# Hashed attention with a convolved feed-forward layer: reciprocals spread by two transposes, and queries and keys loaded head by head

## The chip, the cores and the metric

The kernel runs on one core of a Trainium2 chip. A core has a matmul engine (PE, with its weight loads shown apart as PEld), a vector engine (DVE), a scalar engine (ACT), a general engine (POOL) and a queue for transfers (SP). Each works through its own instructions in order, and semaphores tie them together. The metric is the device time of one execution in microseconds (us); lower is better.

## The reference

Four batches of eight heads, 768 positions, head size 64. Queries and keys are hashed to six sign bits; a query attends only to keys of its own bucket. The attention's output, the heads side by side, goes through a feed-forward layer with a convolution over three positions that gates the hidden values.

```python
q_bits = (np.einsum('bhsd,dk->bhsk', q, proj) > 0).astype(np.int64)
...
mask = q_bucket[:, :, :, None] == k_bucket[:, :, None, :]
scores = scale * np.matmul(q, k.transpose(0, 1, 3, 2))
scores = np.where(mask, scores, -1000000000.0)
scores = scores - np.max(scores, axis=-1, keepdims=True)
attn = np.exp(scores)
attn = attn / (np.sum(attn, axis=-1, keepdims=True) + 1e-09)
return np.matmul(attn, v).astype(np.float32)
...
h = np.maximum(x @ w_in, 0.0)
...
    conv_out += conv_w[k][None, None, :] * hp[:, k:k + S, :]
gate = 1.0 / (1.0 + np.exp(-conv_out))
return (h * gate @ w_out).astype(np.float32)
```

## The kernel before

Heads are worked on in pairs: sixteen pairs (`Pair`), four per batch. A pair has twelve units (`Unit`), each 128 queries of one head against all 768 keys. After the last pair of a batch, three pairs delayed (`DEFER`), comes that batch's feed-forward stage (`ffn`).

A unit goes through four steps. `products` (L257): the scores, in four matmuls into a PSUM tile `s`; the values are split into a high and a low part, and the hash bits ride along as additional rows, so that a wrong bucket gives a large negative score. `maximum` (L270): DVE copies the scores to `e` and takes their maximum. `exponential` (L277): ACT. `transposes` (L297), three units later (`LAG`): PE turns `e`, six blocks of 128 x 128, into a PSUM tile `t`, and ACT copies it to `at` (L304). The tiles `s` and `t` (and that of the hash) are taken in turn from three PSUM buffers, the ring `S`.

Four units make a block of 256 queries for both heads. Its product with the values, `values`, is done in one go behind the last unit of the following block: `spread`, then six chunks for each head (L325). The first seven pairs divide by the sum of the exponentials only there: `reciprocals` (L291, L292) makes four reciprocals per partition on DVE, two units ahead of the burst, and `spread` (L319) turns them into rows, by matmuls with `ident` in which each reciprocal is read 64 times; ACT copies the result to `rs`, and DVE multiplies (L333). The later pairs (`late`) divide each unit's `e` on POOL and have no `spread`.

While a pair runs, the next is prepared. `load` brings R, queries and keys of both heads (L158), with one buffer. `hash` (L186) computes the bits on PE and DVE (L189); `split` makes the high part `hi` on POOL (L171), the low part in place of R (L176), and SP copies both to the tiles that the products read (L174, L178; the target that the profile names `k<-R` is K2). In the main loop, with `k` the unit within the pair, `split` does its four steps at k = 1, 3, 5 and 7, the hash is at k = 3, and at k = 7 SP gets `load_v` for the next pair and then `load` for the one after it. A load of R waits until all readers of the buffer are done, the copies included.

In the background of the first pairs, DVE, ACT and POOL decode the weights of the feed-forward stage, which arrive as 64-bit numbers (L91 to L112), some five steps in each burst.

All the order is written out by hand: each engine has its instructions in the order of the main loop.

Of the kernel before, what the change touches and what calls it, by code (L numbers as in the profile page):

```python
# [17 lines left out]
P = 128  # L18
# [14 lines left out]
LATE = NP + DEFER  # L33
AVS = (1 + NCK, 0, 0, 0)
PREP = 1
PREP_N = 6
W0 = 7
RATE = 5.2
WC = 512
# [3 lines left out]
def lsh_attention_conv_ffn(ctx, tc, qk, v, hw, w_in, conv_w, w_out, consts, ident_in, out):  # L43
# [100 lines left out]
    class Pair:  # L144
        def __init__(self, b, p):
            self.b, self.p, self.nm = b, p, f"{b}_{p}"
            self.late = b * NP + p >= LATE
            self.inv = None

        def load(self):  # L150
            nm = self.nm
            self.R = ring(wp, 1, [P, 2, S], F32R, "R", f"R{nm}")
            src = qk[self.b, 2 * self.p:2 * self.p + 2].rearrange("h p s -> p h s")
            if self.b == self.p == 0:
                for h in range(2):
                    nc.sync.dma_start(self.R[:, h].bitcast(F32), src[:, h])
            else:
                nc.sync.dma_start(self.R.bitcast(F32), src)  # L158
            self.Q1 = ring(wp, 2, [P, 2, S], F32R, "Q1", f"Q1{nm}")
            self.K1 = ring(wp, 2, [P, 2, S], F32R, "K1", f"K1{nm}")  # L160
            self.Q2, self.K2 = Q2s[self.p % 2], K2s[self.p % 2]
# [4 lines left out]

        def split(self, h):

            lo, R = self.R[:, h], self.R[:, h].bitcast(F32)
            hi = ring(wp, 1, [P, S], F32R, "hi", f"hi{self.nm}_{h}")  # L170
            nc.gpsimd.tensor_scalar(hi, R, 1.0, 0.0, ALU.mult, ALU.add)  # L171
            for dst, src in ((self.Q1[:64, h], hi[:64]), (self.Q2[:64, h], hi[:64]),
                             (self.K1[:64, h], hi[64:]), (self.K1[64:, h], hi[64:])):
                nc.sync.dma_start(dst.bitcast(F32), src.bitcast(F32))  # L174
            yield
            nc.gpsimd.tensor_tensor(lo, R, hi.bitcast(F32), ALU.subtract)  # L176
            for dst, src in ((self.Q1[64:, h], lo[:64]), (self.K2[:64, h], lo[64:])):
                nc.sync.dma_start(dst.bitcast(F32), src.bitcast(F32))  # L178

        def hash(self):  # L180
            hp = ring(ps, 3, [P, 2, 512], F32, "S", f"hash{self.nm}")
            R = self.R.bitcast(F32)
            for h in range(2):
                for half in range(2):
                    g = 32 * (2 * h + half)
                    nc.tensor.matmul(hp[g:g + 32, 0, :HS], hw_sb[:, :32], R[:, h, half * HS:(half + 1) * HS],  # L186
                                     start=True, stop=True, tile_position=(0, g))
# [22 lines left out]
        def prepare_now(self):  # L210

            nm = self.nm
            hps = []
            for h in range(2):
                hps.append(ring(ps, 2, [P, 512], F32, "M", f"hash{nm}_{h}")[:, :HS])
                for g in range(4):
                    c, half = 32 * (1 + g // 2), g % 2
                    nc.tensor.matmul(hps[h][32 * g:32 * g + 32], hw_sb[:, c:c + 32],
                                     self.R[:, h, half * HS:(half + 1) * HS].bitcast(F32),
                                     start=True, stop=True, tile_position=(0, 32 * g))  # L220
            for h in range(2):
                R = self.R[:, h].bitcast(F32)
                Q1, Q2, K1, K2 = (t[:, h] for t in (self.Q1, self.Q2, self.K1, self.K2))
                nc.gpsimd.tensor_scalar(K1[64:], R[64:], 1.0, 0.0, ALU.mult, ALU.add)
                nc.scalar.copy(K1[:64], R[64:])
                nc.vector.tensor_copy(Q1[:64], R[:64])
                nc.scalar.copy(Q2[:64], R[:64])
                nc.vector.tensor_tensor(Q1[64:], R[:64], Q1[:64].bitcast(F32), ALU.subtract)
                if h == 1:
                    yield  # L230
                bits = ring(wp, 4, [P, WC], I32, "w", f"bits{nm}_{h}").bitcast(F32)[:, :HS]
                nc.vector.tensor_scalar(bits, hps[h], 0.0, cst[:, 2:3], ALU.is_gt, ALU.subtract)
                nc.vector.tensor_tensor(K2[:64], R[64:], K1[64:].bitcast(F32), ALU.subtract)
                for g, dst in enumerate((K2, K2, Q2, Q2)):
                    p, dst = slice(32 * g, 32 * g + 32), dst[64:96, g % 2 * HS:(g % 2 + 1) * HS]
                    if g % 2 == 0:
                        nc.scalar.activation(dst, bits[p], AF.Copy, scale=cst[p, 3:4])  # L237
                    else:
                        nc.gpsimd.tensor_scalar(dst, bits[p], cst[p, 3:4], 0.0, ALU.mult, ALU.add)
            yield  # L240
            nc.vector.tensor_copy(K2s[1][64:96], zero[64:96])
            nc.vector.tensor_copy(Q2s[1][64:96], zero[64:96])


    class Unit:
# [41 lines left out]
        def reciprocals(self):  # L287

            pr = self.pair
            pr.inv = ring(wp, 2, [P, 2 * QB // P], F32, "inv", f"inv{self.nm}")  # L290
            nc.vector.tensor_reduce(pr.inv, self.sums, mybir.AxisListType.X, ALU.add)  # L291
            nc.vector.reciprocal(pr.inv, pr.inv)  # L292

        def transposes(self):
            self.tp = ring(ps, 3, [P, 2, 512], F32, "S", f"t{self.nm}")
# [11 lines left out]
    def values(pr, qb, ats, inv):  # L307
# [7 lines left out]
        def spread():  # L315

            for t in range(QB // P):
                for h in range(2):
                    nc.tensor.matmul(av[h * D:(h + 1) * D, QB + t * P:QB + (t + 1) * P],  # L319
                                     inv[:, 2 * t + h:2 * t + h + 1].to_broadcast([P, D]), ident,  # L320
                                     start=True, stop=True, tile_position=(0, h * D))

        def chunk(c):
            for h in range(2):
# [87 lines left out]
    def ffn(b, xs, fill, last):  # L412
# [4 lines left out]
        for i in range(len(todo) + FLAG):  # L417
# [17 lines left out]
            if i < len(todo):  # L435
# [3 lines left out]
    pairs = [Pair(b, p) for b in range(B) for p in range(NP)]  # L439
    units = [Unit(pr, t, h) for pr in pairs for qb in range(S // QB) for h in range(2)  # L440
             for t in range(qb * QB // P, (qb + 1) * QB // P)]
    pairs[0].load()
    nc.sync.dma_start(ident, ident_in)
    pairs[0].load_v()
    cwr = cp.tile([P, 2 * NFC * 3], I32, name="cwr")
    nc.sync.dma_start(cwr, conv_w)
    first = pairs[0].prepare_now()
    next(first)
    pairs[1].load()
    av, outs, lows, early = [], [], [], None  # L450
    n = len(units)
    ffn_after = {min((b + 1) * NP - 1 + DEFER, B * NP - 1): b for b in range(B)}
    for i in range(n + LAG):
# [53 lines left out]
        for last in parts:  # L507
            last()
        prepare(1)
        if u and k == PREP + PREP_N and pi + 1 < len(pairs):  # L510
            pairs[pi + 1].load_v()
            if pi + 2 < len(pairs):
                pairs[pi + 2].load()
        if i == 3:
            taps.append(decode_taps(cwr))
        for g in taps:
# [64 lines left out]
```

## Time and profile before

| | us |
|---|---|
| median of 3 runs | 740.17 |
| lowest, highest | 739.85, 744.33 |
| profiled execution, whole | 739.48 |
| its span, first to last instruction | 737.5 |

A row of the profile names the line of the code, the engine, the operation, the tile written and those read, and the number of instructions; behind a bar stand the busy time in us, the mean of one in ns, and the idle time of the engine just before, with what ended it. PE's ends are modelled, since matmuls overlap: for them the distance from start to start counts.

| stage, us from the start | what runs |
|---|---|
| 0 to 28 | first pair, loads, start of the decoding |
| 28 to 224 | pairs that use `spread`; decoding of the weights |
| 224 to 290 | feed-forward stage of the first batch |
| 290 to 396 | pairs that divide on POOL |
| 396 to 737.5 | the same by turns: feed-forward, pairs, feed-forward, pairs, feed-forward |

### The profile page before, as it was taken

What the parts mean: (1) busy time and instruction counts of PE and PEld (TensorE: products, weight loads), DVE (VectorE), ACT (ScalarE), POOL (GpSimd) and SP (SyncE); (2) the same over time, 40 slices, a digit from 0 to 9 for tenths busy, and PEclk for the clock granted to TensorE, in tenths of its full rate; (3) what the DMA queues carried; (4) which work ended last, traced back from release to release, by engine and by line L of the source; (5) the groups of instructions that cost most, each with busy time, mean ns of one, the idle gap of its engine ahead of it and who ended that gap; (6) DMA issues with size and microseconds to landing.
All of it is one profiled execution on the core that took longest, in us unless ns stands there. A gap on an engine that the chain in (4) does not pass through costs nothing.

```text
span 737.5 us, 13543 instructions
## 1 busy us (share of the span) xinstructions
PE 710.9 (96%) x4720; PEld 589.0 (80%) x4720; DVE 487.3 (66%) x1211; ACT 498.5 (68%) x937; POOL 331.9 (45%) x334
## 2 busy tenths in 40 slices
PE   6998999899899999999999999999999999999997
PEld 3787777678778988777877998778778899878996
DVE  7977878788775755666665666466666566555663
ACT  5788578678684554877877554778778655585554
POOL 4265456357463522475673532355755232241321
PEclk9999999999999999999999999999999999999999
DMA  4867666663552310237545130324463001100011
GB/s 143 222 187 202 165 186 166 165 166 89 147 146 52 86 44 36 72 77 189 139 105 149 34 94 3 108 60 113 117 180 95 1 0 44 44 1 1 0 44 43
DMA packets 30355, 72.17 MB, mean 98 GB/s; under 512 B 5936, under 2 KB 7504, under 8 KB 30288
## 3 DMA queue, kind: packets, MB, share of 16 engines
q1 hardware_dynamic: 27696, 62.88, 32.0%
q10 hardware_dynamic: 2592, 8.44, 3.3%
q8 instruction: 37, 0.61, 0.3%
q14 instruction: 30, 0.25, 0.1%
HBM read 27.40 MB, written 6.29 MB: 46 GB/s over the span
## 4 chain that ended last, share of the span: by engine, by line
PE 69%; DMA 11%; POOL 7%; issue 5%; DVE 4%; SPq 3%; ACT 1%; POOLq 0%; DVEq 0%; ACTq 0%
PE h L368 19%; PE o L398 18%; PE v L325 11%; PE s L257 10%; PE t L297 9%; DMA R<-in_qk 6%; DMA k<-R 4%; POOL R L176 2%; SPq L174 2%; DVE e L270 1%; DMA K<-hi 1%; PE hash L186 1%; POOL hi L171 1%; ACT e L277 1%; SPq L178 1%
## 5 line engine op out<-in xcount | busy, mean ns | idle before, releaser
L270 DVE TENSOR_SCALAR_CACHE_REDUCE e<-s 128x768 f32<-128x768 f32 x192 | 183.2, 954 | 81.2 <-PE s L257 70.6
L277 ACT ACTIVATE e<-e,st 128x768 f32<-128x768 f32 x192 | 181.3, 944 | 10.3 <-DVE st L284 5.0
L304 ACT COPY at<-t 128x768 f32<-128x768 f32 x192 | 152.3, 794 | 47.0 <-PE t L297 47.0
L297 PE MATMUL t<-ident,e 128*128 128x128 f32 x1152 | 160.0, 275 | 3.6 <-POOL e L285 1.5
L377 DVE SCALAR_TENSOR_TENSOR ht<-ht,cw 128x384 f32<-128x384 f32 (+1 forms) x128 | 114.7, 896 | 71.2 <-ACT ht L375 69.0
L387 POOL TENSOR_TENSOR g<-ht,g 128x384 fp32r<-128x384 f32 x64 | 71.5, 1117 | 179.5 <-ACT g L386 141.8
L297 PEld LDWEIGHTS t<-ident,e 128*128 128x128 f32 x1152 | 130.6, 141 | 22.3 <-POOL e L285 7.4
L285 POOL TENSOR_SCALAR e<-e,st 128x768 f32<-128x768 f32 x108 | 98.3, 911 | 103.1 <-DVE st L284 51.4
L398 PE MATMUL o<-wo,g 128*128 128x512 f32 x576 | 142.4, 394 | 0.0
L368 PE MATMUL h<-xh,wi 128*128 128x386 f32 x512 | 141.9, 340 | 0.0
L325 PE MATMUL v<-at,v 128*64 128x256 f32 x1152 | 135.6, 385 | 0.0
L398 PEld LDWEIGHTS o<-wo,g 128*128 128x128 f32 x576 | 107.4, 188 | 20.3
L257 PE MATMUL s<-K,Q 128*128 128x384 f32 x384 | 116.7, 385 | 1.9 <-ACT e L277 1.0
L325 PEld LDWEIGHTS v<-at,v 128*64 128x64 f32 x1152 | 81.2, 138 | 42.4 <-issue 8.6
L257 PE MATMUL s<-k,q 96*128 96x384 f32 x384 | 100.2, 342 | 2.1 <-ACT q L237 1.9
L368 PEld LDWEIGHTS h<-xh,wi 128*128 128x128 f32 x512 | 94.1, 188 | 4.8 <-issue 1.8
L380 ACT ACTIVATE ht<-ht 128x384 f32<-128x384 f32 x64 | 33.6, 526 | 91.4 <-DVE ht L377 91.4
L368 PE MATMUL h<-xl,wi 128*128 128x386 f32 x256 | 86.7, 339 | 0.0
L257 PEld LDWEIGHTS s<-K,Q 128*128 128x128 f32 x384 | 59.0, 192 | 23.2 <-issue 16.6
L257 PEld LDWEIGHTS s<-k,q 96*128 96x128 f32 x384 | 70.7, 191 | 3.5 <-ACT q L237 3.0
L381 DVE TENSOR_TENSOR ht<-ht 128x384 f32<-128x384 f32 x64 | 40.2, 629 | 33.4 <-ACT ht L380 33.4
L176 POOL TENSOR_TENSOR R<-R,hi 128x768 fp32r<-128x768 f32 x30 | 56.6, 1886 | 0.2
(75 smaller groups left out, 586.0 us busy)
## 6 DMA issues: line engine op xcount, KB each, us to landing
R<-in_qk SPq DMA_DIRECT2D x15, 768.0 KB
K<-hi SPq DMA_DIRECT2D x60, 192.0 KB
v<-in_v SPq DMA_DIRECT2D x16, 384.0 KB
out<-osb SPq DMA_DIRECT2D x24, 256.0 KB
Q<-hi SPq DMA_DIRECT2D x30, 192.0 KB
q<-hi SPq DMA_DIRECT2D x30, 192.0 KB
Q<-R SPq DMA_DIRECT2D x30, 192.0 KB
k<-R SPq DMA_DIRECT2D x30, 192.0 KB
```

Source lines behind the costliest of these rows:

```text
L176: nc.gpsimd.tensor_tensor(lo, R, hi.bitcast(F32), ALU.subtract)
L257: nc.tensor.matmul(self.sp[:, half, :HS], A[:, h, qs], C[:, h, half * HS:(half + 1) * HS], start=(kk == 0), stop=(kk == 1))
L270: nc.vector.tensor_scalar(self.e.rearrange("p (a b) -> p a b", a=2), self.sp[:, :, :HS], MASKED, None, ALU.max, ALU.max, accum_out=self.st ...
L277: nc.scalar.activation(self.e, self.e, AF.Exp, bias=self.st[:, 1:2], scale=SCALE, accum_out=self.sum)
L285: nc.gpsimd.tensor_scalar(self.e, self.e, self.st[:, 3:4], 0.0, ALU.mult, ALU.add)
L297: nc.tensor.transpose(self.tp[:, c // 3, c % 3 * P:(c % 3 + 1) * P], self.e[:, c * P:(c + 1) * P], ident)
L304: nc.scalar.copy(pr.at[self.h][:, :, :, self.tq * P:(self.tq + 1) * P], self.tp[:, :, :3 * P].rearrange("p j (c q) -> p j c q", c=3))
L325: nc.tensor.matmul(av[h * D:(h + 1) * D, :QB], vt[:, c, h, :], ats[h][:, c // 3, c % 3, :], start=(c == 0), stop=(c == NCK - 1), tile_posi ...
L368: nc.tensor.matmul(hp[:, :HW], w, x[:, c0:c0 + HW], start=(n == 0), stop=(n == 3 * NCC - 1))
L377: nc.vector.scalar_tensor_tensor(t[:, a:z], ht[:, o + k - 1 + a:o + k - 1 + z], cw[:, f, k:k + 1], t[:, a:z], ALU.mult, ALU.add)
L387: nc.gpsimd.tensor_tensor(g[:, 1, :], t, g[:, 0, :].bitcast(F32), ALU.subtract)
L398: nc.tensor.matmul(op, l, r, start=(f == 0 and n == 0), stop=(f == NFC - 1 and n == 2))
```

## The change

Two things. The reciprocals are written out 64 times each: DVE sums into a tile `total` and then makes a tile `inv` of 128 x 256, by reading each total 64 times; `spread` is then two transposes of 128 x 128 in place of four times two matmuls with 64 columns. And R becomes a tile for each head with a load for each, the first at k = 7, the second at k = 8, where `load_v` now stands behind them.

```diff
-PREP_N = 6
+PREP_N = 6,7
...
-        def load(self):
+        def load(self, h):
+
             nm = self.nm
-            self.R = ring(wp, 1, [P, 2, S], F32R, "R", f"R{nm}")
-            src = qk[self.b, 2 * self.p:2 * self.p + 2].rearrange("h p s -> p h s")
-            if self.b == self.p == 0:
-                for h in range(2):
-                    nc.sync.dma_start(self.R[:, h].bitcast(F32), src[:, h])
-            else:
-                nc.sync.dma_start(self.R.bitcast(F32), src)
+            self.R[h] = ring(wp, 1, [P, S], F32R, f"R{h}", f"R{nm}_{h}")
+            nc.sync.dma_start(self.R[h].bitcast(F32), qk[self.b, 2 * self.p + h])
+            if h == 0:
+                return
...
         def reciprocals(self):
 
             pr = self.pair
-            pr.inv = ring(wp, 2, [P, 2 * QB // P], F32, "inv", f"inv{self.nm}")
-            nc.vector.tensor_reduce(pr.inv, self.sums, mybir.AxisListType.X, ALU.add)
-            nc.vector.reciprocal(pr.inv, pr.inv)
+            total = ring(wp, 2, [P, 2 * QB // P], F32, "total", f"total{self.nm}")
+            nc.vector.tensor_reduce(total, self.sums, mybir.AxisListType.X, ALU.add)
+
+            pr.inv = ring(wp, 1, [P, QB], F32, "inv", f"inv{self.nm}")
+            nc.vector.reciprocal(pr.inv.rearrange("p (a d) -> p a d", d=D),
+                                 total.unsqueeze(2).to_broadcast([P, 2 * QB // P, D]))
...
             for t in range(QB // P):
-                for h in range(2):
-                    nc.tensor.matmul(av[h * D:(h + 1) * D, QB + t * P:QB + (t + 1) * P],
-                                     inv[:, 2 * t + h:2 * t + h + 1].to_broadcast([P, D]), ident,
-                                     start=True, stop=True, tile_position=(0, h * D))
+                nc.tensor.transpose(av[:, QB + t * P:QB + (t + 1) * P], inv[:, t * P:(t + 1) * P], ident)
...
-        if u and k == PREP + PREP_N and pi + 1 < len(pairs):
+        if u and k - PREP in PREP_N and pi + 2 < len(pairs):
+            pairs[pi + 2].load(PREP_N.index(k - PREP))
+        if u and k - PREP == PREP_N[1] and pi + 1 < len(pairs):
             pairs[pi + 1].load_v()
-            if pi + 2 < len(pairs):
-                pairs[pi + 2].load()
```

At the start of the program the second pair's R is loaded by two loads in the same way. The other lines of the diff only change `R[:, h]` to `R[h]`.

On SP's queue, at the end of a pair: what stands before, from the second head's copies to the first copies of the next pair. The number in R's name is the pair's; in `hi` the last small number is the head.

```order
L174 DMA K10_1_125<-hi0_1_1_257 64x768 x2
L178 DMA Q10_1_124<-R0_1_122 64x768
L178 DMA k2_1_82<-R0_1_122 64x768
L165 DMA v0_1_335<-in_v 128x768
L158 DMA R0_2_337<-in_qk 128x2x768
L174 DMA Q10_2_339<-hi0_2_0_498 64x768
```

And the same place in the changed kernel, where R's last small number is the head:

```order
L173 DMA K10_1_128<-hi0_1_1_261 64x768 x2
L177 DMA Q10_1_127<-R0_1_1_125 64x768
L177 DMA k2_1_82<-R0_1_1_125 64x768
L155 DMA R0_2_0_337<-in_qk 128x768
L155 DMA R0_2_1_361<-in_qk 128x768
L164 DMA v0_1_365<-in_v 128x768
L173 DMA Q10_2_363<-hi0_2_0_502 64x768
```

The load of both heads has become two, and `v` has moved behind them.

On DVE, around the reciprocals of the last block of the first pair, in the kernel before (`st` is the unit's small tile for maximum and sum):

```order
L270 TENSOR_SCALAR e0_1_1_0_483,st0_1_1_0_482<-s0_1_1_0_477 128x768
L274 TENSOR_SCALAR st0_1_1_0_482<-st0_1_1_0_482 128x1
L291 TENSOR_REDUCE inv0_0_5_1_486<-sums2_75 128x4
L292 RECIPROCAL inv0_0_5_1_486<-inv0_0_5_1_486 128x4
L270 TENSOR_SCALAR e0_1_0_1_510,st0_1_0_1_509<-s0_1_0_1_504 128x768
```

And in the changed kernel:

```order
L269 TENSOR_SCALAR e0_1_1_0_486,st0_1_1_0_485<-s0_1_1_0_480 128x768
L273 TENSOR_SCALAR st0_1_1_0_485<-st0_1_1_0_485 128x1
L290 TENSOR_REDUCE total0_0_5_1_489<-sums2_75 128x4
L293 RECIPROCAL inv0_0_5_1_491<-total0_0_5_1_489 128x256
L269 TENSOR_SCALAR e0_1_0_1_514,st0_1_0_1_513<-s0_1_0_1_508 128x768
```

The place is the same, between the maxima of two units; the reciprocal writes 256 elements per partition in place of 4.

On PE, the end of that block and the start of the burst with the values, before:

```order
L297 MATMUL t0_1_0_0_533<-ident_66,e0_1_0_0_465 128x128 x6
L186 MATMUL hash0_2_545<-R0_2_337,hw_sb_67 32x384 x4
L319 MATMUL v0_0_2_522<-ident_66,inv0_0_5_1_486 64x128 x4
L325 MATMUL v0_0_2_522<-at0_0_2_0_422,v0_0_91 64x256
L325 MATMUL v0_0_2_522<-at0_0_2_1_423,v0_0_91 64x256
```

And now:

```order
L299 MATMUL t0_1_0_0_537<-ident_66,e0_1_0_0_468 128x128 x6
L185 MATMUL hash0_2_549<-R0_2_0_337,hw_sb_67 32x384 x2
L185 MATMUL hash0_2_549<-R0_2_1_361,hw_sb_67 32x384 x2
L320 MATMUL v0_0_2_526<-ident_66,inv0_0_5_1_491 128x128 x2
L324 MATMUL v0_0_2_526<-at0_0_2_0_427,v0_0_92 64x256
```

Four matmuls of 64 columns have become two of 128 ahead of the same chunks, and the hash reads a tile for each head.

More of the change, by code (lines that the diff above doesn't have):

```diff
@@ L146, in __init__ @@
             self.b, self.p, self.nm = b, p, f"{b}_{p}"
+            self.R = [None, None]
             self.late = b * NP + p >= LATE
             self.inv = None
-        def load(self):
+        def load(self, h):
             nm = self.nm
-            self.R = ring(wp, 1, [P, 2, S], F32R, "R", f"R{nm}")
-            src = qk[self.b, 2 * self.p:2 * self.p + 2].rearrange("h p s -> p h s")
-            if self.b == self.p == 0:
-                for h in range(2):
-                    nc.sync.dma_start(self.R[:, h].bitcast(F32), src[:, h])
-            else:
-                nc.sync.dma_start(self.R.bitcast(F32), src)
+            self.R[h] = ring(wp, 1, [P, S], F32R, f"R{h}", f"R{nm}_{h}")
+            nc.sync.dma_start(self.R[h].bitcast(F32), qk[self.b, 2 * self.p + h])
+            if h == 0:
+                return
             self.Q1 = ring(wp, 2, [P, 2, S], F32R, "Q1", f"Q1{nm}")
@@ L167, in split @@
         def split(self, h):
-            lo, R = self.R[:, h], self.R[:, h].bitcast(F32)
+            lo, R = self.R[h], self.R[h].bitcast(F32)
             hi = ring(wp, 1, [P, S], F32R, "hi", f"hi{self.nm}_{h}")
@@ L181, in hash @@
             hp = ring(ps, 3, [P, 2, 512], F32, "S", f"hash{self.nm}")
-            R = self.R.bitcast(F32)
             for h in range(2):
+                R = self.R[h].bitcast(F32)
                 for half in range(2):
                     g = 32 * (2 * h + half)
-                    nc.tensor.matmul(hp[g:g + 32, 0, :HS], hw_sb[:, :32], R[:, h, half * HS:(half + 1) * HS],
+                    nc.tensor.matmul(hp[g:g + 32, 0, :HS], hw_sb[:, :32], R[:, half * HS:(half + 1) * HS],
                                      start=True, stop=True, tile_position=(0, g))
@@ L218, in prepare_now @@
                     nc.tensor.matmul(hps[h][32 * g:32 * g + 32], hw_sb[:, c:c + 32],
-                                     self.R[:, h, half * HS:(half + 1) * HS].bitcast(F32),
+                                     self.R[h][:, half * HS:(half + 1) * HS].bitcast(F32),
                                      start=True, stop=True, tile_position=(0, 32 * g))
             for h in range(2):
-                R = self.R[:, h].bitcast(F32)
+                R = self.R[h].bitcast(F32)
                 Q1, Q2, K1, K2 = (t[:, h] for t in (self.Q1, self.Q2, self.K1, self.K2))
@@ L441, in lsh_attention_conv_ffn @@
              for t in range(qb * QB // P, (qb + 1) * QB // P)]
-    pairs[0].load()
+    for h in range(2):
+        pairs[0].load(h)
     nc.sync.dma_start(ident, ident_in)
@@ L448, in lsh_attention_conv_ffn @@
     next(first)
-    pairs[1].load()
+    for h in range(2):
+        pairs[1].load(h)
     av, outs, lows, early = [], [], [], None
```

## The prediction, made before the changed kernel ran

> **What bounds the kernel now.** I read the page's busy time by engine first, then busy time by stage, then the stage that the change touches in order of time. The rows below: each engine's busy time with its share of the span; then three stages, each with its length and, by engine, busy time and instructions, then granted clock, DMA share and GB/s.
>
> ```profile
> PE 710.9 (96%) x4720; PEld 589.0 (80%) x4720; DVE 487.3 (66%) x1211; ACT 498.5 (68%) x937; POOL 331.9 (45%) x334
> 28.00:224.00 196.00, 185.49 (x1480) 148.88 (x1480) 156.74 (x404) 148.22 (x277) 103.82 (x107) 0.99 0.60 163
> 290.00:396.00 106.00, 104.76 (x783) 81.89 (x781) 67.13 (x255) 83.24 (x156) 60.51 (x63) 1.00 0.47 124
> 73.40:79.20 5.80, 5.69 (x41) 3.10 (x41) 4.60 (x5) 0.40 (x2) 4.62 (x5) 0.71 0.83 214
> ```
>
> PE (the matmul engine) sets the time: it idles 26.6 of 737.5 us. The change works mostly in the stage from 28 to 224 us, where the weights are decoded on DVE and the first seven pairs are normalised by `spread`. There PE idles 10.5 us, and DVE is busy for 156.7 of 196 us (80%), so DVE is the engine with least room. After 224 us DVE has much more: 67.1 of 106 us.
>
> The idle time of PE by what ended it (total, times, longest), and how one of these waits comes about, first in the chain of waits, then in the order of time of SP's queue and of PE (start, duration, instruction):
>
> ```profile
> PE hash L186 <- DMA R<-in_qk: 9.1, 9, 2.2
> PE hash L186 <- DMA R<-in_qk: 8.3, 7, 2.2
> PE hash L186 <- ACT e L277: 1.3, 2, 0.8
> PE t L297 <- DVE e L270: 1.1, 3, 0.6
> 63.38 3.98 DMA k<-R
> 67.37 6.00 DMA R<-in_qk
> 64.40 0.54 SPq L165 DMA_DIRECT2D v<-in_v  x1
> 67.37 0.39 SPq L158 DMA_DIRECT2D R<-in_qk  x1
> 73.51 0.85 PE L186 MATMUL hash<-R,hw_sb 128*32 128x384 f32 x8 [2.18 <-DMA R<-in_qk]
> 74.29 0.66 PE L319 MATMUL v<-ident,inv 128*64 128x128 f32 x8
> 74.78 4.45 PE L325 MATMUL v<-at,v 128*64 128x256 f32 x24
> ```
>
> The second row is that view cut at 224 us: 8.3 of the 9.1 us lie in the early stage. The single buffer R can only be loaded when the DMA that copies the last half out of it (k<-R) is done; that DMA, then 768 KB, then the hash. The worst wait also left the clock at 0.71 for the next 5.8 us (stage row above): the `v` burst took 4.45 us, 1.7 more than the 2.76 of an undisturbed one, quoted next.
>
> **The change part by part.** The next rows are one block of four units: PE, then DVE.
>
> ```profile
> 50.82 0.84 PE L297 MATMUL t<-ident,e 128*128 128x128 f32 x6
> 51.44 0.62 PE L257 MATMUL s<-K,Q 128*128 128x384 f32 x2
> 51.89 0.52 PE L257 MATMUL s<-k,q 96*128 96x384 f32 x2
> 52.25 0.82 PE L297 MATMUL t<-ident,e 128*128 128x128 f32 x6
> 52.99 0.66 PE L319 MATMUL v<-ident,inv 128*64 128x128 f32 x8
> 53.48 2.76 PE L325 MATMUL v<-at,v 128*64 128x256 f32 x24
> 51.02 0.18 DVE L292 RECIPROCAL inv<-inv 128x4 f32<-128x4 f32 x1
> 51.12 0.93 DVE L270 TENSOR_SCALAR_CACHE_REDUCE e<-s 128x768 f32<-128x768 f32 x1
> 52.44 0.96 DVE L270 TENSOR_SCALAR_CACHE_REDUCE e<-s 128x768 f32<-128x768 f32 x1 [0.20 <-PE s L257]
> 57.19 0.96 DVE L270 TENSOR_SCALAR_CACHE_REDUCE e<-s 128x768 f32<-128x768 f32 x1 [0.67 <-PE s L257]
> ```
>
> *Spread by two transposes.* Before, `spread` holds PE from 52.99 to 53.48: 0.49 us. A transpose of the same shape costs what one of a `t` group costs: from the group's start to the next instruction is 0.62 us (50.82 to 51.44) for six, 0.10 each, so two hold PE for 0.20. `t` to `spread` is 0.74, some 0.15 of it the change of array shape; the transposes have the shape of `t`, so this change moves behind them and stays single. Saved: 0.29 us. Where a hash stands between `t` and `spread` (six of the 21 places), the array goes from the hash's shape to 128 columns and then to 64, one change more, so only about 0.1 is saved. Sum: 15 x 0.29 + 6 x 0.1 = 5.0 us off PE. All of it lies on PE's path.
>
> *The reciprocal.* It goes from 4 to 256 elements per partition. No row shows that form. The nearest:
>
> ```profile
> L284 DVE RECIPROCAL st<-st 128x1 f32<-128x1 f32 x108 | 17.5, 162 | 0.0
> L292 DVE RECIPROCAL inv<-inv 128x4 f32<-128x4 f32 x21 | 3.7, 178 | 0.7
> L281 DVE TENSOR_SCALAR st<-st 128x1 f32<-128x1 f32 x108 | 16.5, 153 | 15.0 <-ACT e L277 14.7
> L333 DVE TENSOR_TENSOR rs<-v,rs 128x256 f32<-128x256 f32 x21 | 8.7, 416 | 2.1 <-ACT rs L330 2.1
> ```
>
> An ordinary instruction costs (416 - 153) / 255 = 1.03 ns per further element, 152 ns fixed. At that price the new one takes 0.42 us: the lower bound. But three further elements of a reciprocal cost 16 ns, not 3: 5.3 ns each, which makes 178 + 252 x 5.3 = 1.52 us. Measured from the fixed cost of the ordinary instruction, the four cost (178 - 152) / 4 = 6.5 ns each: 1.82 us. The one-element row gives 10 ns for its single element, 2.7 us: the upper bound. I take the middle of the two estimates from the four-element row, which is nearest: 1.67 us, 1.49 more than now.
>
> DVE is strictly in order, and behind this instruction stands the maximum of the next unit (51.12). The PSUM tiles of `s` and `t` take turns in three buffers, so the `t` group of 52.25 writes where the `s` read by that maximum stood: PE waits for it, and everything behind it on PE (spread, `v`, the next products) waits too. That this wait is real, the next rows show: in one place the maximum started at 29.85, ended at 30.80, and `t` started 0.05 later after an idle 0.59 us. In the block above the maximum ends at 52.05 and `t` starts at 52.25, so 0.15 us is free. The third row is the place with most room, where PE itself came 1.15 us late.
>
> ```profile
> 29.85 0.95 DVE L270 TENSOR_SCALAR_CACHE_REDUCE e<-s 128x768 f32<-128x768 f32 x1
> 30.86 0.87 PE L297 MATMUL t<-ident,e 128*128 128x128 f32 x6 [0.59 <-DVE e L270]
> 129.90 0.96 DVE L270 TENSOR_SCALAR_CACHE_REDUCE e<-s 128x768 f32<-128x768 f32 x1 [1.15 <-PE s L257]
> ```
>
> Read in the same way, 16 of the 21 places have 0.14 to 0.24 us free, five have 0.3 to 1.35; together 6.2 us. Cost on PE: 21 x 1.49 - 6.2 = 25.1 us. Behind the burst the DVE had 0.67 us to spare in this block (57.19) because it decodes weights while PE works on `v`. DVE moves later by about 0.3 us more than PE does (1.29 after regaining the 0.20 at 52.44, against 1.34 - 0.29 = 1.05). In some six blocks that spare time is zero already; there the next maximum comes later too: 1.3 us in all. Sum 26.4 us. By the lower bound (0.24 us more each, mostly inside the free time) it is about 1 us; by the upper bound 25.1 + 21 x 1.03 + 1.3 = 48 us.
>
> The Trainium skill (VectorE: DVE Perf Modes, section on the fixed hardware budget) says that a reciprocal is an iterated division with a repeat count of 8, on an engine clocked at 0.96 GHz. Read as eight cycles per element that would be an estimate of 8.3 ns, 2.3 us for the instruction and a sum some 13 us higher; the trace's 5.3 to 6.5 ns speak for less, its 10 ns of the single element for more.
>
> *The loads.* The first head's tile no longer waits for the second head's copies: its load is issued at 64.4, where the `v` load stood, right behind the issue of k<-R. The second head's load still waits for k<-R as R did (67.37), but brings 384 KB instead of 768, and nothing of `v` in front. So the hash's data should be complete 1 to 3 us sooner. Besides, the hash now comes two long reciprocals later after that DMA, some 2 us. Either is enough for nearly every wait (mean 9.1 / 9 = 1.0, longest 2.2). I take the whole of the 9.1 us, and the 1.7 us of the slow burst: 10.8 us saved. The 1.3 us put down to `e` may be the same thing, but I leave it out. The bounds: nothing saved, or 12.1. The `v` load goes behind both on SP's queue, some 3 us later than before; its first reader stands twelve units further on, over 25 us, so that costs nothing. POOL's `hi` of the first head can start sooner; POOL is busy 45% and gains nothing for PE. SP issues one DMA more per pair, 0.4 us on a queue that mostly waits.
>
> **Sum:** 26.4 - 5.0 - 10.8 = +10.6 us on the profiled run's 739.5 (its span 737.5 and 2.0 around it, 0.7 under the median of the runs): 750.1 us.
>
> **The rivals.** *The reciprocal is cheap* (0.42 us, as L333's elements): 1 - 5.0 - 10.8 = -14.8, so 724.7 us, faster. For it: same engine, same number of elements, and many of DVE's instructions run at that price. Against it: 16 ns for three elements. This decides the sign: with 5.0 + 10.8 - 1.3 = 14.5 us of gains to be used up, break-even lies where 21 times the addition less 6.2 makes 14.5, an addition of 0.99, at 1.16 us per instruction, 3.9 ns per element.
>
> *It comes out even:* 5.3 ns per element (21 x 0.15 = 3.1 us less) and the hash waits put down to `e` go too (1.3 less): 745.7 us, within 1%. For it: the slope of the two reciprocal rows, the only one with nothing else in it.
>
> *The reciprocal is dearer*, halfway between the 6.5 and the 10 ns, 8.25: 152 + 256 x 8.25 = 2.26 us, 21 x 0.59 = 12.4 us more: 762.5 us. For it: the one-element row. Against it: the four-element row should then read 152 + 33 = 185, not 178. (The Trainium skill's page on the VectorE, read as above, would give nearly this case.)
>
> *The loads don't help,* since the second head waits for the same DMA: 10.8 us are not saved, 760.9 us. Against it: half the bytes, and a hash that comes later.
>
> **How the numbers follow.** About 1%, 7.4 us, is what a measurement of this kernel can tell from no change: 732.8 to 747.6 counts as the same. The forecast as summed 0.42, even 0.27, cheap 0.17, dearer 0.10, loads don't help 0.04. Slower: 0.42 + 0.10 + 0.04 = 0.56; same 0.27; faster 0.17. The time is that of the likeliest case, 750. The range goes from 735 to 764: it leaves out the cheap case and a little of the dearer one. The forecast's own range is 747.7 to 756.
>
> **What would show it.** In the profile after, the RECIPROCAL of 128x256 has a row of its own: near 1.7 us right, under 1.2 the sign is wrong. PE's `t` should have a wait for DVE's `e` of some 20 us, against 1.1 now; the hash's wait for R should be nearly gone; the transposes of `inv` should stand 42 times, and PE should go from them to `v` in 0.2 us a pair plus a change of shape; the burst behind each hash should be near 2.76 us with the clock at 1.0. Wrong would be: a short reciprocal; `t` not waiting, because the maximum's tile is free sooner than I read it; or a new wait of PE for something whose row is nearly zero here, such as POOL's `bits` or the copies into `k`.

## The result, and the profile after

| | before | changed |
|---|---|---|
| median, us (4 runs each) | 740.78 | 752.62 |
| lowest, highest | 739.85, 744.33 | 750.77, 754.09 |
| profiled execution, whole | 739.48 | 751.17 |
| its span | 737.5 | 749.4 |

The ratio of the times is 1.015, with a 95% interval from 1.0104 to 1.0195: the changed kernel is slower, by 11.8 us at the median. The forecast was 750.1.

First the page of the changed kernel: busy time by engine, then the shares of the chain that ended last; the third row is that chain in the kernel before.

```profile
PE 708.2 (95%) x4594; PEld 582.0 (78%) x4594; DVE 514.5 (69%) x1211; ACT 500.4 (67%) x937; POOL 331.2 (44%) x334
PE 80%; DVE 14%; ACT 2%; DMA 1%; issue 1%; POOL 1%; ACTq 0%; DVEq 0%; POOLq 0%
PE 69%; DMA 11%; POOL 7%; issue 5%; DVE 4%; SPq 3%; ACT 1%; POOLq 0%; DVEq 0%; ACTq 0%
```

PE has 2.7 us less to do than before (710.9), in 126 matmuls fewer, and idles 41.2 us in place of 26.6. DVE has 27.2 us more to do, and 14% of the chain is now its own, against 4%; the share of DMA has gone from 11% to 1%. The new instruction has this row (shortest, median and longest in ns, then the first and the last start):

```profile
L293 DVE RECIPROCAL inv<-total x21: 1752/1753/1755, 22.3 to 234.0; 128x256 f32<-128x256 f32 x21
```

That is 1.75 us each time, 1.575 more than the 178 ns of the four-element form. What ended PE's idle time, in the view that the prediction read of before (total, times, longest):

```profile
PE t L299 <- DVE e L269: 25.9, 24, 1.3
PE hash L217 <- DMA hw_sb<-in_hw: 4.3, 1, 4.3
...
PE v L324 <- ACT at L306: 1.5, 1, 1.5
```

The wait of `t` for the maximum has gone from 1.1 to 25.9 us. The wait of the hash of L185 for R (9.1) has no row any more, nor has the 1.3 put down to `e`. The hash of L217, the first pair's own, waits for its weights as before (4.4). New is one wait of `v` for `at`, in the first pair; e1 below shows what it is. One block in order of time, PE and then DVE:

```profile
98.50 0.52 PE L256 MATMUL s<-k,q 96*128 96x384 f32 x2
100.27 0.87 PE L299 MATMUL t<-ident,e 128*128 128x128 f32 x6 [1.25 <-DVE e L269]
100.98 0.38 PE L320 MATMUL v<-ident,inv 128*128 128x128 f32 x2
101.29 2.81 PE L324 MATMUL v<-at,v 128*64 128x256 f32 x24
104.03 0.62 PE L256 MATMUL s<-K,Q 128*128 128x384 f32 x2
```

```profile
97.64 1.75 DVE L293 RECIPROCAL inv<-total 128x256 f32<-128x256 f32 x1
99.31 0.90 DVE L269 TENSOR_SCALAR_CACHE_REDUCE e<-s 128x768 f32<-128x768 f32 x1
100.32 0.95 DVE L269 TENSOR_SCALAR_CACHE_REDUCE e<-s 128x768 f32<-128x768 f32 x1
...
103.71 0.43 DVE L95 TENSOR_SCALAR lowi<-lowi 128x512 int32<-128x512 int32 x1
105.04 0.96 DVE L269 TENSOR_SCALAR_CACHE_REDUCE e<-s 128x768 f32<-128x768 f32 x1 [0.90 <-PE s L256]
```

The maximum cannot start before the reciprocal is done (99.31), ends at 100.21, and `t` starts 0.06 later, after an idle 1.25 us. Behind the burst DVE has 0.90 us to spare (105.04): it is late at one place of the block only, and PE pays for that place in 20 of the 21 blocks. From the start of the last matmul of `t` to the next products are 3.16 us, as the median of 14 plain blocks, against 3.38 in the kernel before: the transposes save 0.22. The windows' row of the early pairs (length; busy time of PE, PEld, DVE, ACT, POOL; granted clock, DMA share, GB/s) shows that the clock stays at 1.00 in spite of the waits:

```profile
28.00:236.00 208.00, 183.21 (x1366) 141.95 (x1367) 182.34 (x402) 149.96 (x277) 100.34 (x103) 1.00 0.57 154
```

The next table puts the same work side by side, as the first start of a feed-forward matmul splits each profiled execution. All the reciprocals and all but the last use of them lie ahead of it.

| us | ahead of the first feed-forward matmul | from there to the end |
|---|---|---|
| before | 220.9 | 516.6 |
| changed | 235.3 (+14.4) | 514.1 (-2.5) |
| e1_loads_only | 217.3 (-3.6) | 514.5 (-2.1) |
| e2_recip_only | 234.6 (+13.7) | 517.5 (+0.9) |
| e3_copy_spread | 222.3 (+1.4) | 514.2 (-2.4) |
| e5_loads_fetch | 212.9 (-8.0) | 514.2 (-2.4) |

The rows of waits count idle time from PE's modelled ends, so they are a little short. The +14.4 is better told by the distances between PE's starts, summed over all places:

| ahead of the first feed-forward matmul, changed less before | us |
|---|---|
| from the products to `t` in the 21 places (31.6 against 3.7) | +27.9 |
| within the six matmuls of `t` there | +1.1 |
| from the last matmul of `t` to the next products, by the transposes (15 x 0.22, 6 x 0.12) | -4.0 |
| from `t` to the hash, the early waits for R | -8.5 |
| the burst that was slow at 74.78 | -1.7 |
| the first burst, with the new wait of `v` | +2.1 |
| from `t` to other products | -2.2 |

Together +14.7; the rest is in small pieces. The last row is other waits of PE, above all one of 1.0 us for ACT's `e`, which the changed kernel doesn't have. Of the -2.5 behind the first feed-forward matmul, 2.1 are the late part of the hash's waits, 0.8 for R and 1.3 put down to `e`.

### The profile page after: what moved, and what is told of

Same layout as the page of the kernel before. It is cut to its first block, busy times and chain, and to the rows that moved or that the text cites. A ratio compares the mean times of both kernels' runs of the same rounds, so it can differ in the third digit from the quotient of the medians.

```text
span 749.4 us, 13352 instructions
## 1 busy us (share of the span) xinstructions
PE 708.2 (95%) x4594; PEld 582.0 (78%) x4594; DVE 514.5 (69%) x1211; ACT 500.4 (67%) x937; POOL 331.2 (44%) x334
## 4 chain that ended last, share of the span: by engine, by line
PE 80%; DVE 14%; ACT 2%; DMA 1%; issue 1%; POOL 1%; ACTq 0%; DVEq 0%; POOLq 0%
PE h L367 18%; PE o L397 18%; PE v L324 16%; PE t L299 13%; PE s L256 12%; DVE e L269 6%; DVE inv L293 4%; ACT at L306 2%; PE hash L185 2%; DMA Q<-R 1%; PE v L320 1%; DVE st L273 1%; DMA R<-in_qk 0%; ACT e L276 0%; POOL e L284 0%
## 5 line engine op out<-in xcount | busy, mean ns | idle before, releaser
L299 PE MATMUL t<-ident,e 128*128 128x128 f32 x1152 | 161.0, 276 | 28.1 <-DVE e L269 25.9
L299 PEld LDWEIGHTS t<-ident,e 128*128 128x128 f32 x1152 | 128.9, 141 | 52.6 <-DVE e L269 33.5
L324 PEld LDWEIGHTS v<-at,v 128*64 128x64 f32 x1152 | 79.4, 137 | 46.9 <-issue 11.0
```

Source lines behind the costliest of these rows:

```text
L299: nc.tensor.transpose(self.tp[:, c // 3, c % 3 * P:(c % 3 + 1) * P], self.e[:, c * P:(c + 1) * P], ident)
L324: nc.tensor.matmul(av[h * D:(h + 1) * D, :QB], vt[:, c, h, :], ats[h][:, c // 3, c % 3, :], start=(c == 0), stop=(c == NCK - 1), tile_posi ...
```

## The experiments

Two theories stood at the start. The one of the prediction: the long reciprocal in front of a maximum makes PE wait, and the rest of the change is a gain. Its rival: the loads, or the transposes, bring less than they seem to, and the reciprocal less loss. All kernels compute the whole reference. Diffs are against the changed kernel unless said otherwise; ratios are to the kernel before, run on the same chip.

### e1_loads_only: the reciprocals and `spread` as before, the loads as changed

```diff
-            nc.vector.reciprocal(pr.inv.rearrange("p (a d) -> p a d", d=D),
-                                 total.unsqueeze(2).to_broadcast([P, 2 * QB // P, D]))
+            nc.vector.reciprocal(pr.inv, pr.inv)
...
-                nc.tensor.transpose(av[:, QB + t * P:QB + (t + 1) * P], inv[:, t * P:(t + 1) * P], ident)
+                for h in range(2):
+                    nc.tensor.matmul(av[h * D:(h + 1) * D, QB + t * P:QB + (t + 1) * P],
+                                     inv[:, 2 * t + h:2 * t + h + 1].to_broadcast([P, D]), ident,
```

> The loads alone: a tile and a load for each head, reciprocals and spread as before. Theory: the loads are worth the hash waits by themselves, 9.1 + 1.3 us of idle PE and 1.7 us of a slow burst, so about 12 us off the profiled 739.5: 727 to 730 us, ratio near 0.985, and no wait of the hash for R over 0.2 us. Rival: in the changed kernel the waits are gone because the long reciprocals make the hash come later; without these the second head's data still comes late, half of the waits stays, 733 us or more.

Measured: 733.36 us (6 runs) beside 741.68 (17 runs), ratio 0.988 (0.985 to 0.9909). The loads alone are a gain of 8.3 us. The hash's wait is gone from the list, as forecast, but not all of it is gone. In three of the six early pairs the second head's matmuls start 0.4 to 0.84 us behind the first head's, where 0.01 is usual: 1.9 us in all, of the 8.5 that stood there before. PE's modelled ends hide this; the weight loads show it, here for the pair at 75.82:

```profile
76.47 0.14 PEld L185 LDWEIGHTS hash<-R,hw_sb 128*32 128x32 f32 x4 [0.51 <-DMA R<-in_qk]
```

So the rival of the expectation holds to a small part. And a wait of `v` has come. The list's row of it, from the profile of this kernel:

```profile
PE v L324 <- ACT at L303: 2.5, 1, 2.5
```

It stands in the first pair. ACT in order of time there (ACTq is its sequencer, which issues the transfers of the weights):

```profile
24.39 0.19 ACT L276 ACTIVATION_READ_ACCUMULATOR e<-e,st 128x1 f32 x1
27.57 0.34 ACTq L132 DMA_DIRECT2D rawi<-in_w_in  x1
27.95 0.80 ACT L303 COPY at<-t 128x768 f32<-128x768 f32 x1 [3.37 <-DMA Q<-R]
```

And PE's burst, then the window of that burst (length, busy time and instructions of PE, PEld, DVE, ACT, POOL, granted clock, DMA share, GB/s):

```profile
28.80 4.49 PE L324 MATMUL v<-at,v 128*64 128x256 f32 x22 [2.47 <-ACT at L303]
```

```profile
28.80:33.20 4.40, 4.40 (x22) 2.28 (x22) 1.36 (x4) 2.49 (x5) 0.00 (x0) 0.61 0.96 288
```

ACT stood 3.37 us in front of the issue of a weight load, which reads nothing that Q<-R writes. In the trace the transfers take eight completion semaphores (the flags that tell of a landing) by turns. This load has the one last used by Q<-R, issued at 20.77, and waits for it; in the kernel before, with one load less ahead of it, it had the one of an earlier weight load. The copy to `at` is queued behind the issue, and PE waits for the copy: 2.5 us, and then 1.7 more because the clock fell to 0.61 and the burst took 4.49 us rather than 2.76. The changed kernel has the same wait of ACT, 3.70 us for Q<-R, and the smaller one of PE, 1.48 us, behind which the burst stayed fast (2.80 us).

### e2_recip_only: the reciprocals and transposes as changed, the loads as before

```diff
-            self.R[h] = ring(wp, 1, [P, S], F32R, f"R{h}", f"R{nm}_{h}")
-            nc.sync.dma_start(self.R[h].bitcast(F32), qk[self.b, 2 * self.p + h])
+            self.R = ring(wp, 1, [P, 2, S], F32R, "R", f"R{nm}")
...
-        if u and k - PREP in PREP_N and pi + 2 < len(pairs):
-            pairs[pi + 2].load(PREP_N.index(k - PREP))
-        if u and k - PREP == PREP_N[1] and pi + 1 < len(pairs):
+        if u and k == PREP + PREP_N and pi + 1 < len(pairs):
             pairs[pi + 1].load_v()
+            if pi + 2 < len(pairs):
+                pairs[pi + 2].load()
```

> The reciprocals and transposes alone, R loaded as before. Theory: the hash now comes about 2 us later after the DMA that frees R, so most of its waits go without the new loads, and the time is near that of the whole change, 750 to 755 us. Rival: the loads are what removed the waits, and they are back here: 760 to 764 us, with 8 us or more of the hash waiting for R.

Measured: 752.69 us (6 runs), ratio 1.0142 (1.0119 to 1.0166): the same as with the loads. From this kernel's list of waits:

```profile
PE t L300 <- DVE e L270: 26.4, 26, 1.3
...
PE hash L186 <- DMA R<-in_qk: 3.2, 5, 1.2
```

Four of the five waits for R lie after the first feed-forward stage, and the early one is 0.17 us. So ahead of it these waits go whatever the loads do: a hash that comes later finds its data there. The third hash of the loop, for instance, comes 7.25 us behind the issue of R (71.63 to 78.88), where before it came after 6.14 and had waited (67.37 to 73.51). The prediction had said that either cause would be enough; beside the long reciprocal it is the lateness, and the loads add nothing there. What they bring in the changed kernel is the late part (table above: 3.4 us less after the first feed-forward matmul than here) and they cost 0.7 ahead of it. These 2.7 us are 0.4%, less than the intervals of the two ratios tell apart.

### e3_copy_spread: four reciprocals, then a copy on DVE that repeats each 64 times

```diff
-            nc.vector.reciprocal(pr.inv.rearrange("p (a d) -> p a d", d=D),
-                                 total.unsqueeze(2).to_broadcast([P, 2 * QB // P, D]))
+            nc.vector.reciprocal(total, total)
+            nc.vector.tensor_copy(pr.inv.rearrange("p (a d) -> p a d", d=D),
+                                  total.unsqueeze(2).to_broadcast([P, 2 * QB // P, D]))
```

> The whole change, but DVE takes four reciprocals per partition as before and a copy repeats each 64 times. Theory: the cost of the change is the long reciprocal alone; the copy takes 0.3 to 0.45 us and 1 to 5 us of it reach PE, the transposes save 5: 723 to 729 us, a little under the loads alone. Rival: the wait of the transposes for the maximum comes from the additional tile and its place and not from the reciprocal's length, or the transposes bring nothing: 733 us or more.

Measured: 738.23 us (12 runs), ratio 0.9947 (0.9925 to 0.9968). Most of the loss is gone, but the time is 9 us above the expectation's end. The row of the copy, from this kernel's trace:

```profile
L293 DVE COPY inv<-total x21: 293/418/1837, 22.8 to 220.5; 128x256 f32<-128x256 f32 x21
```

The same instruction takes 0.29 us at best and 1.84 at worst. One of the long ones, with the engines mixed in order of time:

```profile
54.62 1.84 POOL L175 TENSOR_TENSOR R<-R,hi 128x768 fp32r<-128x768 f32 x1
...
55.25 1.37 DVE L293 COPY inv<-total 128x256 f32<-128x256 f32 x1
...
56.54 0.95 DVE L269 TENSOR_SCALAR_CACHE_REDUCE e<-s 128x768 f32<-128x768 f32 x1
...
57.55 0.66 PE L299 MATMUL t<-ident,e 128*128 128x128 f32 x4 [1.15 <-DVE e L269]
```

It ends 0.16 us after POOL's instruction (56.46), and PE pays 1.15 us, almost as much as for the long reciprocal. The others agree: of the 21 copies the 14 that take over 0.3 us all start while an instruction of POOL runs, of one input or of two, and end 0.14 to 0.16 us behind it. The Trainium skill (SBUF — State Buffer, section on the two separate sides) describes a pair of ports that DVE and POOL share and that one holds for a whole instruction while the other stands. The trace agrees in these ends; the 1.753 us of the reciprocal, within 3 ns in all 21 places, 19 of them beside POOL's work, show that it isn't held up in that way. In this kernel's list `t` waits 6.2 us for the maximum, 11 times; by PE's starts the 21 places take 8.7 us more than before, where 1 to 5 had been expected. The first pair loses its 4 us as in e1 (`v` waits 2.5 us for `at`, and a slow burst follows), and the transposes save 4 in place of 5. These make most of the missed 9.

### e4_twice: the long reciprocal done twice

```diff
+            nc.vector.reciprocal(pr.inv.rearrange("p (a d) -> p a d", d=D),
+                                 total.unsqueeze(2).to_broadcast([P, 2 * QB // P, D]))
```

> The whole change with the long reciprocal done twice in a row, the second with the same result. Theory: DVE's free time ahead of the maximum is used up, so nearly each further us of DVE at that place is an us of PE: 21 x 1.7 = 35 us more than the whole change, 785 to 790 us, and the wait of t for e grows from 26 to near 60 us. Rival: DVE's delay is taken up by the burst behind it and the changed kernel's loss has another source: under 770 us.

Measured: 815.88 us in a single run, 63 above the changed kernel's median. From its list of waits, and its stage of the early pairs in the columns of the windows:

```profile
PE t L301 <- DVE e L269: 61.9, 22, 3.4
```

```profile
28.00:288.00 260.00, 202.06 (x1302) 149.74 (x1302) 209.01 (x404) 144.34 (x263) 94.89 (x96) 0.88 0.45 120
```

The wait grew by 36.0 us, 1.71 for each of 21 instructions of 1.75: nothing hides a second one. The time grew by more, because the clock over this stage fell from 1.00 to 0.88. One place, from PE's order of time:

```profile
190.82 1.54 PE L301 MATMUL t<-ident,e 128*128 128x128 f32 x6 [2.87 <-DVE e L269]
...
192.72 4.86 PE L326 MATMUL v<-at,v 128*64 128x256 f32 x24
```

After an idle 2.87 us the same `t` takes 1.54 us rather than 0.87 and the burst 4.86 rather than 2.81. After the changed kernel's 1.25 us they don't. But it isn't so in every place of this kernel:

```profile
109.99 0.88 PE L301 MATMUL t<-ident,e 128*128 128x128 f32 x6 [2.79 <-DVE e L269]
...
111.02 2.81 PE L326 MATMUL v<-at,v 128*64 128x256 f32 x24
```

Of 20 such waits, of 2.79 to 3.45 us, five are followed by a `t` and a burst at full pace, so the length of the wait alone doesn't decide.

### e5_loads_fetch: e1, with the third weight load issued one unit earlier

Against e1:

```diff
-        fetch(i % 2 if i < 8 else burst)
+        fetch(i in (1, 3, 4, 7) if i < 8 else burst)
```

> The loads alone (as the first experiment), and of the first four weight loads on ACT's queue the third one unit earlier, so that it no longer stands behind the copy Q<-R of the second pair. Theory: the loads alone lost 4 us again in the first pair, because ACT's queue stood 3 us at that weight load until Q<-R had landed (PE idle 2.5 us, then a burst at a lower clock); without it 727 to 731 us, 3 to 5 under the loads alone, and no wait of v for at over 0.5 us. Rival: the transfers of the first pair saturate the DMA engines anyway and the wait moves to another instruction: within 1.5 us of the loads alone.

Measured: 730.57 us (6 runs) beside 742.85 (11 runs), ratio 0.9836 (0.9795 to 0.9876), the shortest time of all. From its list of waits, the row of the hash's weights with all that stands under it in the first rows:

```profile
PE hash L217 <- DMA hw_sb<-in_hw: 4.4, 1, 4.4
PE s L256 <- ACT q L236: 1.9, 1, 1.9
PE s L256 <- DMA Q<-R: 1.5, 2, 1.2
```

`v` no longer waits for `at`. The wait for the semaphore of Q<-R is now one of SP's (a copy of `bits`, issued at 27.34), and ACT stands only 1.97 us, at the fourth weight load; PE pays for neither. From the first hash of the loop to the second are 26.37 us, against 30.61 in e1 and 26.04 before. So the order of the transfers was the cause of e1's lost 4.2 us, and the loads with it mended gain some 12.

### e6_act_copy and e7_act_fetch: four reciprocals, repeated by ACT

Here DVE keeps its four reciprocals, and ACT writes the 256 elements, behind the exponential of the same step; the transposes and the loads stay. e7 has the earlier weight load too.

```diff
+            nc.vector.reciprocal(self.total, self.total)
+        def repeat(self):
...
+            nc.scalar.copy(pr.inv.rearrange("p (a d) -> p a d", d=D),
+                           self.total.unsqueeze(2).to_broadcast([P, 2 * QB // P, D]))
...
+        if two and not two.pair.late and two.tq == QB // P - 1 and two.h == 1:
+            two.repeat()
```

> The whole change, but four reciprocals per partition as before, and ACT repeats each 64 times, behind the exponential. Theory: the DVE's copy in the third experiment was slow (0.29 to 1.84 us) because it stood still while POOL worked; ACT's copy takes 0.37 us each time, ACT has over 1 us to spare in each block, and the transposes save 5 us: 726 to 730 us, 4 to 6 under the loads alone. Rival: the transposes bring PE nothing, or ACT becomes the bound of the block: 733 us or more.

> The copy on ACT and the earlier weight load together. Theory: the two gains add: 722 to 726 us. Rival: one takes the place of the other, 727 us or more.

Measured: e6 733.99 us (6 runs), ratio 0.987 (0.9829 to 0.9912), with e1's wait of `v` for `at` of 2.5 us; e7 731.02 (6 runs), 0.9838 (0.9797 to 0.988). That is e1 and e5 again: no gain by the transposes can be measured. ACT and PE in e7, in order of time:

```profile
91.88 0.40 ACT L296 COPY inv<-total 128x256 f32<-128x256 f32 x1
92.17 0.80 ACT L309 COPY at<-t 128x768 f32<-128x768 f32 x1
```

```profile
92.56 0.38 PE L323 MATMUL v<-ident,inv 128*128 128x128 f32 x2
92.87 2.96 PE L327 MATMUL v<-at,v 128*64 128x256 f32 x24
95.76 0.63 PE L256 MATMUL s<-K,Q 128*128 128x384 f32 x2
```

The copy on ACT costs 0.29 us from start to start and stands in front of the last `at` of the burst, which is done at 92.97, when the burst has begun. The second head's part then comes late: from the burst to the next products are 2.89 us, against 2.74 in the changed kernel. Two more of PE's waits for ACT stand in e7's list:

```profile
PE s L256 <- ACT at L309: 1.8, 2, 1.3
...
PE hash L185 <- ACT at L309: 1.5, 5, 0.3
```

The longest, 1.3 us, has e1's cause once more: in the first pair ACT stands 3.55 us in front of the fourth weight load, which was not moved. From the first burst to the second e7 takes 10.70 us, e5 8.89. But over the other 19 distances from burst to burst, too, e7 has no gain: 181.1 us against 180.7.

### e8_later: the long reciprocal two units later, in the burst, and the transposes at its end

```diff
-        return [spread, *chunks], (factors, out, parts)
+        return [*chunks, spread], (factors, out, parts)
...
-        two = units[i - 2] if 2 <= i <= n + 1 else None
-        if two and not two.pair.late and two.tq == QB // P - 1 and two.h == 1:
-            two.reciprocals()
+        for back in (2, 4):
+            x = units[i - back] if back <= i < n else None
...
+                x.reciprocals()
```

> The whole change with the same long reciprocal, but two units later: behind the maximum of the burst's unit, with the transposes at the burst's end in place of its start. Theory: what the change costs is the place ahead of a maximum that PE waits for; in the burst DVE has some 0.7 us to spare in two blocks of three, so 0.3 to 0.7 us of each 1.2 go: 737 to 747 us, and t's wait for e falls to under 20 us. Rival: DVE's total in a block is the bound and the place plays no part: 750 to 754 us.

Measured: 761.85 us (6 runs, 757.27 to 767.22), ratio 1.0255 (1.0206 to 1.0303): slower still, where a gain was expected. From its list of waits, and DVE in order of time:

```profile
PE t L299 <- DVE e L269: 27.0, 19, 3.1
```

```profile
91.31 1.75 DVE L293 RECIPROCAL inv<-total 128x256 f32<-128x256 f32 x1
92.98 0.36 DVE L332 TENSOR_TENSOR rs<-v,rs 128x256 f32<-128x256 f32 x1
93.26 0.68 DVE L101 SCALAR_TENSOR_TENSOR lowi<-rawi,lowi 128x512 f32<-128x512 uint32 x1
...
94.77 1.48 DVE L95 TENSOR_SCALAR lowi<-lowi 128x512 int32<-128x512 int32 x1
96.29 1.63 DVE L97 SCALAR_TENSOR_TENSOR upi<-rawi,lowi 128x512 int32<-128x512 int32 x1
97.84 0.94 DVE L269 TENSOR_SCALAR_CACHE_REDUCE e<-s 128x768 f32<-128x768 f32 x1
```

DVE has no gap from 91.31 to the maximum at 97.84: the five steps of decoding now stand behind the reciprocal, two of them at 1.48 and 1.63 us where the changed kernel's block has 0.43 for L95, and `t` waits 3.06 us for that maximum. The 0.90 us that DVE had to spare behind the burst are less than 1.75, and some of the steps now fall beside POOL's work (POOL has instructions of 1.3 us from 94.68 and from 96.05). So the place alone was not the fault: in neither of the two places tried has DVE room for the further 1.58 us. The row of `t` is only 1.1 us above that of the changed kernel, though, while the part ahead of the first feed-forward matmul is 5.9 us longer (241.2); the rest is spread over several waits, and why the median is 9 us higher was not settled.

### e9_act_end: e7, with ACT's copy behind the last `at` and the transposes at the burst's end

Against e7:

```diff
-        if two and not two.pair.late and two.tq == QB // P - 1 and two.h == 1:
-            two.repeat()
...
+            if not w.pair.late and w.tq == QB // P - 1 and w.h == 1:
+                w.repeat()
...
-        return [spread, *chunks], (factors, out, parts)
+        return [*chunks, spread], (factors, out, parts)
```

> The seventh experiment with ACT's copy one unit later, behind the copy of the block's last t, and the transposes at the burst's end. Theory: in the seventh the transposes' gain was lost because ACT's copy stood ahead of the copy of the block's last t, for which the values' matmuls of the second head wait; now t to the next s should take 3.1 to 3.2 us in place of 3.3 and of 3.38 without transposes, and the time should be 3 to 5 us under that of the fifth: ratio 0.977 to 0.980. Rival: ACT is so late in the block that its 0.39 us reach PE wherever they stand: a ratio of 0.983 or more, as the fifth and seventh.

Measured: 731.46 us (6 runs) beside 742.4 (11 runs), ratio 0.9849 (0.9813 to 0.9884), no better than e5 or e7. Plain blocks do become shorter, 8.6 us from burst to burst against 8.9 in e5. From `t` to the next products are 3.19 us, as expected. But from the first burst to the 21st are 193.3 us, against 189.6 in e5, and two longer waits stand in its list:

```profile
PE s L256 <- ACT at L309: 3.0, 2, 1.7
...
PE t L302 <- DVE e L269: 1.2, 4, 0.5
```

Of the 3.7 us, 3.5 lie between the first burst and the second (12.35 us against 8.89). There ACT stands once more in front of the fourth weight load:

```profile
33.17 0.37 ACT L332 COPY rs<-v 128x256 f32<-128x256 f32 x1 [3.84 <-DMA q<-bits]
```

PE waits 1.66 us for `at` behind it, and the clock over the next 4.5 us is 0.62. So the first pair hides what the place of ACT's copy is worth. The other 19 distances are 180.9 us against 180.7: what the plain blocks gain is lost again in other places, mostly blocks with a hash, and to what was not settled.

## Why the prediction was right

*The bound.* The forecast rested on one step: the maximum of the next unit is queued behind the reciprocal, and PE waits for that maximum because `t` needs its buffer. The wait appeared at that place, 25.9 us in total against 1.1, where the sum had 25.1 of added waiting. e4 shows that it is this instruction: a second one added 36.0 us to the same row. e2 shows that the new loads aren't needed for the loss, and e3 and e6, which keep the transposes with four reciprocals, that most of it goes with the long reciprocal.

*The size of the reciprocal.* 1.753 us against 1.67. Less the 153 ns of an ordinary instruction this is 1.600 us for 256 elements, 6.25 ns each: within 4% of the 6.5 that the fixed-cost reading of the four-element row gave, and 17% above the 5.3 of the slope, so the middle was a little low. The cheap rival (0.42 us) and the dear one (2.26) both fall by this row. Of the 10 ns of the single element only some 6 are its price, the rest is fixed cost. The Trainium skill's repeat count of 8 (VectorE: DVE Perf Modes, the fixed hardware budget), read as eight cycles, had given an estimate of 8.3 ns; the measurement says 6.25, which would be six cycles at the 0.96 GHz that the same page states (its Specifications).

*The free time.* With the measured length the sum would have had 21 x 1.575 - 6.2 = 26.9 us of waiting. The list has 24.8 more; by PE's starts it is 27.9. One of the 21 places, the last, lies in the feed-forward stage and pays nothing; the other 20 pay 1.40 each, so 0.18 us was free in each of them. That is what the prediction read in most places; the one with 1.3 us of room, where PE came late for another reason, lost it as that reason went. The six matmuls of `t` take another 1.1 us in all, which no term had. What the prediction added for DVE being late behind the burst (1.3 us) is no row of its own in the profile after.

*The transposes.* 4.0 us against 5.0: 0.22 in place of 0.29 in a plain block, and 0.12 in place of 0.1 beside a hash. Right in place, a little too large; the burst behind them is 0.05 us longer (2.74 from start to start, against 2.69). In e6, e7 and e9, where ACT writes the 256 elements, no gain was left in the whole time.

*The loads.* This is the term whose total came out nearly (10.8 expected; 12.3 went: 8.5 early, 1.7 of the slow burst, 2.1 late) while its cause was only half right. The 1.3 put down to `e`, which it had left out, are in the late part. The prediction named two causes, either of which would do, and booked the gain to the loads. e2 shows that in the changed kernel the later hash alone removes the early waits, and e1 that without the long reciprocal the loads remove most of them, 1.9 us staying between the two heads. The rival that the loads don't help would have been 10.8 us slower only if the lateness did nothing either; it did.

*What was missed.* The loads' place in the order of all transfers. One transfer more at the start moved the third weight load onto the completion of Q<-R and cost PE 2.1 us in the changed kernel (1.5 in the list) and 4.2 in e1, with the slow clock. The prediction costed the additional DMA by the 0.4 us of its issue on SP and didn't look at who issues the other transfers; it had only said that a new wait of PE would be a sign against it.

*The sum.* Against the profiled execution +10.6 us were forecast, and +11.7 came (its span +11.9). The terms, forecast and measured: waiting for the maximum 26.4 and 29.0 (with the 1.1 in `t`), transposes -5.0 and -4.0, loads -10.8 and -12.3; and, not forecast, the missed wait 2.1 and the other waits of the products -2.2. The measured ones make 12.6, and 0.7 less is in small pieces. The sign and the place are no luck; that the total came within 1.3 us is partly luck, since errors of up to 2.6 us in the terms cancel.

## What to carry to other kernels

A loss and a gain were tied together here: one head's load at a time, with one weight load issued earlier, is worth 12 us (e5), and the 256-element reciprocal costs more than that, because 1.6 us of a strictly ordered engine stand in front of the instruction for which PE waits. Before an operation is widened to save work on the bounding engine, take its price per element from the smallest rows there are, less the fixed cost of a plain instruction, and compare it with the free time of the next instruction in the queue, not with the engine's mean load (DVE was busy 80% of this stage, and in neither of the two places tried did the other 20% lie where they could be used). After any change in the number of transfers look again at the first waits of every engine that issues them: here such a wait came back in e1, e3 and e6 to e9. And where a list says that PE's wait is gone, check the distances between its starts.

## What the runs showed of the hardware

- A reciprocal on DVE: 153 ns and 6.25 ns per element, the same to within 3 ns whatever POOL does (21 instances).
- A copy on DVE of the same 256 elements: 0.29 us, and up to 1.84 where an instruction of POOL runs as it starts; it then ends 0.14 to 0.16 us behind that instruction (e3).
- Behind idle times of PE of 2.18 us (before), 2.47 (e1) and 2.87 (e4) the clock was lower (0.71 and 0.61 over what followed the first two, and a burst of 4.86 us in e4); behind 1.25 and 1.48 us, and behind 1.82 and 1.87 in the kernel before, the burst was fast, and so it was in e4 behind five of 20 waits of 2.79 to 3.45. The Trainium skill (TensorE: Matmul & The Clock Gate, section on what is actually happening) gives an idle window of about 3.4 us that runs freely; here shorter gaps were enough in some places, so the figure can't be taken as a safe length.
- A transfer's issue can wait for an unrelated earlier transfer: 3.37 us on ACT in e1. Moving that issue by one unit took the wait to where PE did not pay for it in e5; in e7 and e9 ACT stood 3.55 and 3.84 us at the next weight load.
